# Transposing q and k by halves of the tokens, and reading a recurrent state with 64-row matmuls

## The chip, the cores and the metric

The kernel runs on one core of a Trainium2 chip. The metric is the time of one execution on the device, in microseconds (us); the median of five executions is given. A separate profiled execution of the same program gives the profile and the trace, on which all readings rest.

The core's engines work side by side: TensorE (PE; its weight loads are shown apart as PEld), VectorE (DVE), ScalarE (ACT), GpSimd (POOL) and SyncE (SP), which here only starts DMA transfers. PSUM is the memory that matmuls write; its banks are named psX, psZ, psWH and psO below.

## What is computed

A gated linear recurrence over 768 tokens for 4 batches of 8 heads with 48 dimensions, and behind it a two-layer network with a squared ReLU:

```python
for t in range(S):
    state = alpha[:, :, t, :, None] * state + np.einsum('bhd,bhe->bhde', k[:, :, t], v[:, :, t])
    y[:, :, t] = np.einsum('bhd,bhde->bhe', q[:, :, t], state)
x = y.transpose(0, 2, 1, 3).reshape(B * S, H * D)      # 3072 x 384
out = np.maximum(x @ w_in, 0.0) ** 2 @ w_out           # 384 -> 2048 -> 384
```

## The kernel before

The work is cut into 12 units of 256 tokens of one batch (line 354: the first 256 tokens of the four batches are units 0 to 3, the next are 4 to 7, and so on). The recurrence inside a unit is computed by chunks. Tokens lie in pairs: partition p holds tokens 2p and 2p+1 (index j), and the unit has two chunks c, the partitions 0 to 63 and 64 to 127, each with 128 tokens. A unit goes through these steps:

- `load` (493): alpha, k, q and v go from DRAM into RAW, 384 KB each. Most loads start on SyncE's queue. From unit 5 on each load waits for a step of the unit before (`BEHIND`, line 491): alpha for `ln`, k for the landing of the first transpose `tr0_`, q and v for that of the second, `tr1_`. From unit 4 on it also waits for the landing of the previous unit's q (line 988).
- `front` (673): logarithms of alpha, summed along the tokens by a matmul (`m1`), become the factors EK and EQ; k and q times these go into QKS (line 694, bfloat16, each head padded from 48 to 64, so that two heads fill 128 columns). QKS is then transposed into KQT, so that dimensions lie on partitions. Units 0 to 2 do it with TensorE and a copy out of PSUM; from unit 3 on two DMA transposes on SyncE's queue do it (line 721), one for k (a=0) and one for q (a=1), each of a 128 x 1024 source.
- `scores` (810): 32 matmuls of 64 x 64 tiles give k times q for each chunk, head and token pair (line 827), into psX and psZ. VectorE multiplies them with the causal mask into PM (line 840).
- `output` (846) with `output_mm` (751): psX collects the result. First, q times the state: chunk 0 reads the old state SBD, chunk 1 the middle state SMD. These are 16 matmuls of 128 rows and 64 columns of the array (line 764), a pair of heads at a time, 96 columns each; since two heads share the rows, the blocks of the state that mix them must be zero. For units 0 to 3 there is no old state, and 8 matmuls remain. Then 32 matmuls of 64 rows (line 771) add PM times v, chunk c from the row tile c, into chunk c's bank. In the same piece of TensorE's program stand the next unit's state products (`state_mm`, line 744).
- `state` (782): VectorE adds the state products of the first chunk to SBD (into TMP[0], line 797), and POOL or VectorE masks out the mixed blocks (by OWN, lines 799 and 801) into SMD. Then the second chunk is added (TMP[1], line 804) and scaled by the decay, with mixed blocks set to zero (806 and 808), into SBD. For units 0 to 3 the masking is done in one step (794).
- ScalarE copies psX into XBF (858). Units 4 to 10 transpose XBF by a DMA (879), the others by TensorE (873).
- `moe` (911): the first layer takes 48 matmuls of 256 columns (930), ReLU and squares run on ACT and DVE (938 to 952), and the second layer takes 32 matmuls of 384 columns (966); copies and stores follow (973 to 976).

No loop runs on the chip: a planner (`Program.schedule`, 101) orders every engine's instructions when the program is built. Each operation has an engine or a choice of engines, an assumed cost, a due time, and the buffers that it reads and writes; the planner plays these through and takes at each point the ready operation that is due first. Due times are a multiple of 13 us per unit, but for the first units they come from the tables FRONT, ATTN and DENSE (357 to 359). An operation waits at run time, on its engine's queue, for the operations it depends on, and all that is planned behind it on that engine waits with it. Where TensorE has nothing to do before the first second-layer matmul, matmuls with zeros fill in (1010).

Of the kernel before, what the change touches and what calls it, by code (L numbers as in the profile page):

```python
# [6 lines left out]
ALU = mybir.AluOpType  # L7
# [326 lines left out]
def bass_gla_recurrent__then__act_relu_squared_kernel(  # L334
# [22 lines left out]
    FRONT = {0: 0, 1: 15124, 2: 28243, 3: 27962, 4: 36918, 5: 52460}  # L357
    ATTN = {1: 12619, 2: 26150, 3: 37152, 4: 50460}
    DENSE = {0: 20223, 1: 32105, 2: 46275, 3: 57124, 11: 158500}
# [4 lines left out]
    TR_RING = "sp"  # L364
    LATE_STATE = (1, 2)
    BY_HEADS = (0,)
# [124 lines left out]
    BEHIND = {"a": "ln", "k": "tr0_", "q": "tr1_", "v": "tr1_"}  # L491
# [181 lines left out]
    def front(g):  # L673
# [19 lines left out]
        for a, E, key in ((0, EK, "ek"), (1, EQ, "eq")):  # L693
# [5 lines left out]

        for a in range(2):  # L700
            src = QKS[qs][:, a].rearrange("p j h d -> p (j h d)")
            if g < PE_TRANSPOSED:
                bank = psZ[:, a, :].bitcast(BF16)
                psk = [("ps", "Z", a)]

                def tr(pe, src=src, bank=bank):
                    for o in range(2 * NPR):
                        ins = pe.matmul(bank[:, o * 128:(o + 1) * 128], src[:, o * 128:(o + 1) * 128], IDENT[:],
                                        is_transpose=True)
                    return ins  # L710

                add("pe", tr, pe_ns(8, 128), p0 + 2500 + a, reads=[("qks", qs, a), ("ident",)], writes=psk,
                    name=f"tr{a}_{g}")
                dst = KQT[kt][:, a].rearrange("p j n s -> p (j n s)")
                add("dve", lambda e, dst=dst, bank=bank: e.tensor_copy(dst, bank[:, 0:1024]), dve_ns(1024, 2),  # L715
                    p0 + 3000 + a, reads=psk, writes=[("kqt", kt, a)], name=f"et{a}_{g}",
                    alts={"act": (lambda e, dst=dst, bank=bank: e.activation(dst, bank[:, 0:1024], AF.Copy),
                                  act_ns(1024))})
            else:
                dst = KQT[kt][:, a].rearrange("p j n s -> p (j n) s")  # L720
                add(TR_RING, lambda e, dst=dst, src=src: e.dma_start_transpose(dst, src), 1300, p0 + 2500 + a,
                    reads=[("qks", qs, a)], writes=[("kqt", kt, a)], name=f"tr{a}_{g}", dma=f"t{a}_{kt}", lag=1700)
# [319 lines left out]
```

## Time and profile before

| what | value |
|---|---|
| median of 5 executions | 180.24 us (179.4 to 180.63) |
| profiled execution | 180.24 us, of which 178.4 in the span from first to last instruction |
| first layer on TensorE (L930) | 576 matmuls of 256 columns, busy 74.5 us |
| second layer on TensorE (L966) | 368 matmuls of 384 columns, busy 69.0 us |
| state read (L764) | 160 matmuls, 128 x 64 of the array |
| PM times v (L771) | 384 matmuls, 64 x 128 of the array |
| DMA transposes of QKS (L721) | 18, landing 4.4 us after issue (median; 3.2 to 6.0) |
| loads of RAW | 2.7 to 6.8 us to landing, median 4.8 |

The profile's busy times add the full lengths of single matmuls, which overlap in TensorE's pipeline; what a group of matmuls takes of TensorE is read from the starts of the groups. The profile gives the DMA engines' load as a mean over all 16.

### The profile page before, as it was taken

The numbers are of one execution on the slowest core, as the hardware profiler recorded it, in microseconds if no ns is written. First come the engines' busy times: TensorE is split into PE (matmuls) and PEld (weight loads), VectorE is DVE, ScalarE is ACT, GpSimd is POOL, SyncE is SP. The second block draws the span as 40 slices with busy tenths as digits, with TensorE's granted clock in tenths as the row PEclk, the third lists the DMA queues.
The fourth block names the chain that finished last, engine by engine and source line by source line (L and its number), as shares of the span: only waits on it lengthen the run. The fifth ranks groups of instructions, "written<-read, shape, count | busy, mean of one in ns | idle before, by whom it ended". The sixth has DMA issues, their size and how long they took to land.

```text
span 178.4 us, 5228 instructions
## 1 busy us (share of the span) xinstructions
PE 171.8 (96%) x2287; PEld 136.6 (77%) x2287; DVE 121.4 (68%) x197; ACT 120.1 (67%) x211; POOL 25.8 (14%) x35
## 2 busy tenths in 40 slices
PE   7699899999999999999999999999999999999994
PEld 5577698866778689678878877878788697798773
DVE  6379589789968987869959937848858646342130
ACT  5566289686699786658779757858787664475541
POOL 3060654320002204001102110100100100000000
PEclk9999999999999999999999999999999999999999
DMA  4999999998999898879999997698979930110112
GB/s 123 251 324 185 209 331 208 218 253 242 225 272 215 231 175 208 240 163 212 224 256 201 194 288 183 142 287 121 237 193 241 216 94 5 44 48 0 44 48 88
DMA packets 74615, 33.18 MB, mean 186 GB/s; under 512 B 69888, under 2 KB 73088, under 8 KB 74592
## 3 DMA queue, kind: packets, MB, share of 16 engines
q1 hardware_dynamic: 72944, 27.73, 68.5%
q0 software_dynamic: 1648, 5.11, 12.8%
q8 instruction: 18, 0.29, 0.7%
q14 instruction: 5, 0.04, 0.1%
HBM read 25.17 MB, written 4.72 MB: 168 GB/s over the span
## 4 chain that ended last, share of the span: by engine, by line
PE 81%; DMA 11%; SPq 3%; ACT 2%; issue 1%; POOL 1%
PE psO L966 34%; PE psWH L930 33%; DMA raw<-in_alpha_dram 6%; DMA win<-in_moe_w_in_dram 5%; PE psX L771 3%; PE psX L764 2%; SPq L514 2%; PE psX L827 2%; PE psZ L744 2%; PE psX L900 1%; PE psZ L827 1%; PE psWH L632 1%; ACT gt L952 1%; POOL prd L625 1%; PE psX L873 1%
## 5 line engine op out<-in xcount | busy, mean ns | idle before, releaser
L930 PE MATMUL psWH<-xt,win 128*128 128x256 bf16 x576 | 74.5, 275 | 0.8 <-DMA win<-in_moe_w_in_dram 0.8
L930 PEld LDWEIGHTS psWH<-xt,win 128*128 128x128 bf16 x576 | 64.9, 145 | 6.0 <-DVE kqt L715 1.0
L966 PE MATMUL psO<-wout,gt 128*128 128x384 bf16 x368 | 69.0, 326 | 0.1
L938 ACT ACTIVATE rr<-psWH 128x512 bf16<-128x512 f32 x85 | 50.4, 595 | 25.6 <-PE psWH L930 24.4
L966 PEld LDWEIGHTS psO<-wout,gt 128*128 128x128 bf16 x368 | 35.3, 98 | 17.8 <-ACT osb L973 0.3
L948 DVE TENSOR_TENSOR gt<-rr 128x1024 bf16<-128x1024 bf16 (+1 forms) x43 | 24.2, 572 | 20.2 <-ACT rr L938 20.0
L973 ACT ACTIVATE osb<-psO 128x384 f32<-128x384 f32 x20 | 9.8, 490 | 11.0 <-PE psO L966 10.4
L952 ACT ACTIVATE gt<-rr 128x1024 bf16<-128x1024 bf16 (+1 forms) x17 | 15.8, 931 | 0.6 <-DVE rr L940 0.2
L840 DVE TENSOR_TENSOR pm<-psZ,caus 128x1024 bf16<-128x1024 f32 x12 | 14.6, 1216 | 2.1 <-PE psZ L827 2.1
L840 DVE TENSOR_TENSOR pm<-psX,caus 128x1024 bf16<-128x1024 f32 x12 | 14.6, 1218 | 1.5 <-PE psZ L827 1.5
L858 ACT ACTIVATE xbf<-psX 128x768 bf16<-128x768 f32 x11 | 8.9, 811 | 5.9 <-PE psZ L744 4.5
L1010 PE MATMUL psO<-zero 128*128 128x256 bf16 x72 | 11.1, 303 | 1.2 <-DVE zero L426 1.2
L690 POOL CAST vbf<-raw 128x768 bf16<-128x768 f32 x6 | 5.1, 847 | 43.6 <-DMA raw<-in_v_dram 43.6
L797 DVE TENSOR_TENSOR tmp<-psZ,sbd 128x384 f32<-128x384 f32 x8 | 4.5, 558 | 10.2 <-PE psZ L744 10.1
L694 DVE TENSOR_TENSOR qks<-raw,eq 128x768 bf16<-128x768 f32 x11 | 10.5, 953 | 1.2 <-DMA raw<-in_q_dram 0.6
L694 DVE TENSOR_TENSOR qks<-raw,ek 128x768 bf16<-128x768 f32 x11 | 10.5, 951 | 0.6 <-DMA raw<-in_k_dram 0.6
L1010 PEld LDWEIGHTS psO<-zero 128*128 128x128 bf16 x72 | 7.4, 108 | 2.7 <-DVE zero L426 1.2
L940 DVE TENSOR_SCALAR rr<-psWH 128x512 bf16<-128x512 f32 x11 | 7.5, 686 | 1.7 <-PE psWH L930 1.6
L771 PE MATMUL psX<-vbf,pm 64*128 64x48 bf16 x384 | 6.9, 180 | 0.0
L806 POOL TENSOR_TENSOR sbd<-tmp,acm 128x384 bf16<-128x384 f32 x4 | 4.2, 1048 | 18.3 <-DVE tmp L804 18.1
L653 DVE TENSOR_TENSOR ek<-ek,raw 128x384 f32<-128x384 f32 x9 | 6.0, 668 | 0.9 <-ACT ek L644 0.7
L644 ACT ACTIVATE ek<-psWH 128x384 f32<-128x384 f32 x10 | 4.9, 490 | 2.0 <-PE psWH L636 2.0
(120 smaller groups left out, 164.8 us busy)
## 6 DMA issues: line engine op xcount, KB each, us to landing
out_dram<-osb SPq DMA_DIRECT2D x23, 192.0 KB, 2.9
raw<-in_k_dram SPq DMA_DIRECT2D x11, 384.0 KB, 4.3
raw<-in_q_dram SPq DMA_DIRECT2D x11, 384.0 KB, 4.8
raw<-in_v_dram SPq DMA_DIRECT2D x10, 384.0 KB, 5.7
raw<-in_alpha_dram SPq DMA_DIRECT2D x10, 384.0 KB, 4.4
win<-in_moe_w_in_dram POOLq DMA_DIRECT2D x2, 768.0 KB, 9.7
wout<-in_moe_w_out_dram POOLq DMA_DIRECT2D x2, 768.0 KB, 9.3
raw<-in_v_dram POOLq DMA_DIRECT2D x2, 384.0 KB, 6.3
```

Source lines behind the costliest of these rows:

```text
L694: add("dve", lambda e, a=a, E=E: e.tensor_tensor(QKS[qs][:, a, :, :, 0:D], RAW[r][:, 1 + a].rearrange("p h j d -> p j h d"), E[la][:].rear ...
L771: ins = pe.matmul(psX[:, c, h * D:(h + 1) * D], PM[pm][64 * c:64 * c + 64, n // 2, rr_, n % 2, jk, :], VBF[vb][64 * c:64 * c + 64, h, jk, ...
L840: add("dve", lambda e, hf=hf, psT=psT: e.tensor_tensor(PM[pm][:, hf].rearrange("p r n j t -> p (r n) (j t)"), psT[:, :, :].rearrange("p r ...
L858: add("act", lambda e: e.activation(XBF[x2][:], psX[:, :, 0:HD], AF.Copy), act_ns(2 * HD), p0 + 6100, reads=[("ps", "X", 0), ("ps", "X", 1 ...
L930: ins = pe.matmul(psH[hb][:, i * T:(i + 1) * T], WIN[:, kk, hidden(fj)], mov, start=(kk == 0), stop=(kk == KT - 1))
L938: add("act", lambda e, hb=hb, rr=rr: e.activation(rr, psH[hb], AF.Relu), act_ns(512), pu + 600, reads=[("ps", "H", hb)], writes=[("rr", rb ...
L940: alts={"dve": (lambda e, hb=hb, rr=rr: e.tensor_scalar(rr, psH[hb], 0.0, None, ALU.max), dve_ns(512))})
L948: add("dve", lambda e, dst=dst, sq=sq: e.tensor_tensor(dst, sq, sq, ALU.mult), 148 + k * 267, pu + 1200, reads=[("rr", rb, h) for h in ran ...
L952: "act": (lambda e, dst=dst, sq=sq: e.activation(dst, sq, AF.Square), act_ns(k * 512))})
L966: ins = pe.matmul(psS, GT[gt][:, fj, j, :], WOUT[:, fj, :], start=(fj == 0), stop=(fj == FT - 1))
L973: add("act", lambda e, ob=ob, psS=psS: e.activation(OSB[ob][:], psS, AF.Copy), act_ns(DM), ps_ + 700, reads=[keyS], writes=[("osb", ob)], ...
L1010: pr.fill(lambda pe: pe.matmul(psO[:, 0:256], ZERO[:, 0:128], ZERO[:, 0:256], skip_group_check=True), 109, min(o.start for o in pr.order[" ...
```

## The change

From unit 3 on (`ROW_TILED`):

- The two DMA transposes of a unit each take 64 partitions (one chunk, c) of both k and q: a source of 64 x 2048 in place of 128 x 1024. So both wait for the products of k and of q.
- q is multiplied by its factor in two instructions, one for each j, and laid out so that the transposed q of one chunk and head pair are 128 neighbouring columns.
- The scores read from the new places. Shapes and count stay.
- q times the state becomes 64-row matmuls, a head at a time, 48 columns each, that fill all 128 columns of the array. Row tile x holds the heads 2p+x. [...]the step is cut in two: head parity x writes chunk c = x first; then come the 32 products with v and the next unit's state products; then TensorE waits on a semaphore of its own for the last product with v, and parity x writes chunk c = 1 - x.
- The mixed blocks of SMD are no longer read, so the masking of SMD goes, and the sum is written to SMD directly (for unit 3 a copy). TMP is chosen by the parity of the unit.
- Loads of k wait for the previous unit's product of k (`ekm`), those of q and v for the first of its transposes.
- The due times of units 0 to 5 in FRONT, ATTN and DENSE are changed.

```diff
-    FRONT = {0: 0, 1: 15124, 2: 28243, 3: 27962, 4: 36918, 5: 52460}
-    ATTN = {1: 12619, 2: 26150, 3: 37152, 4: 50460}
-    DENSE = {0: 20223, 1: 32105, 2: 46275, 3: 57124, 11: 158500}
+    FRONT = {0: 0, 1: 13357, 2: 25644, 3: 26390, 4: 37530, 5: 53567}
+    ATTN = {1: 14618, 2: 26767, 3: 37301, 4: 52103}
+    DENSE = {0: 19639, 1: 32250, 2: 48764, 3: 61983, 11: 158500}
...
-    BEHIND = {"a": "ln", "k": "tr0_", "q": "tr1_", "v": "tr1_"}
+    BEHIND = {"a": "ln", "k": "ekm", "q": "tr0_", "v": "tr0_"}
...
+        for j in range(2) if g in ROW_TILED else ():
+            dst = QKS[qs][:, 1].rearrange("p j h d -> p (j h d)").rearrange("p (n j x d) -> p j n x d", n=NPR, j=2, x=2)[:, j, :, :, 0:D]
+            add("dve", lambda e, j=j, dst=dst: e.tensor_tensor(
+                dst, RAW[r][:, 2, :, j, :].rearrange("p (n x) d -> p n x d", x=2),
+                EQ[la][:, j].rearrange("p (n x d) -> p n x d", n=NPR, x=2), ALU.mult),
+                dve_ns(HD), p0 + 1600 + j, reads=[("raw", r, 2), ("eq", la, j)], writes=[("qks", qs, 1, j)], name=f"eqm{j}_{g}")
...
+        if g in ROW_TILED:
+            for c in range(2):
+                src = QKS[qs][64 * c:64 * c + 64].rearrange("p a j h d -> p (a j h d)")
+                dst = transposed(kt, c).rearrange("p (b s) -> p b s", s=64)
+                add("sp", lambda e, dst=dst, src=src: e.dma_start_transpose(dst, src), 1300, p0 + 2500 + c,
+                    reads=[("qks", qs, 0), ("qks", qs, 1)], writes=[("kqt", kt, 0, c), ("kqt", kt, 1, c)], name=f"tr{c}_{g}",
+                    dma=f"t{c}_{kt}", lag=1700)
+            return
...
-                dst = KQT[kt][:, a].rearrange("p j n s -> p (j n) s")
-                add(TR_RING, lambda e, dst=dst, src=src: e.dma_start_transpose(dst, src), 1300, p0 + 2500 + a,
-                    reads=[("qks", qs, a)], writes=[("kqt", kt, a)], name=f"tr{a}_{g}", dma=f"t{a}_{kt}", lag=1700)
...
+    def transposed(kt, c):
+        return KQT[kt][:].rearrange("p a j n s -> p (a j n s)")[:, c * 1024:c * 1024 + 1024]
+
+    def queries(kt, c, n):
+        return transposed(kt, c)[:, 512 + n * 128:512 + n * 128 + 128]
...
+    def output_row_tiled(g, between, between_ns):
...
+        def states(pe, tiles):
+            for p in range(NPR):
+                for x, c in tiles:
+                    h = 2 * p + x
+                    ins = pe.matmul(psX[:, c, h * D:h * D + D], queries(kt, c, p)[64 * x:64 * x + 64],
+                                    (SMD[x2] if c else SBD[sr])[64 * x:64 * x + 64, h * D:h * D + D],
+                                    start=(p == 0 and x == c), stop=False, skip_group_check=True)
+            return ins
+
+        def run(pe):
+            states(pe, ((1, 1),) if first else ((0, 0), (1, 1)))
+            for h in range(H):
...
+            ins.then_inc(swap, 1)
+            swaps[0] += 1
+            if between:
+                between(pe)
+            pe.wait_ge(swap, swaps[0])
+            return states(pe, ((0, 1),) if first else ((0, 1), (1, 0)))
...
+        if g in ROW_TILED and first:
+            add("dve", lambda e: e.tensor_copy(SMD[x2][:], ps0), dve_ns(HD), p0 + 2900,
+                reads=[key0], writes=[("smd", x2)], name=f"sa{g}",
+                alts={"act": (lambda e: e.activation(SMD[x2][:], ps0, AF.Copy), act_ns(HD))})
+        elif g in ROW_TILED:
+            add("dve", lambda e: e.tensor_tensor(SMD[x2][:], ps0, SBD[sr][:], ALU.add), dve_ns(HD),
+                p0 + 2900, reads=[key0, ("sbd", sr)], writes=[("smd", x2)], name=f"sa{g}")
...
-            add("dve", lambda e: e.tensor_tensor(TMP[0][:], ps0, SBD[sr][:], ALU.add), dve_ns(HD),
-                p0 + 2900, reads=[key0, ("sbd", sr)], writes=[("tmp", 0)], name=f"sa{g}")
-            add("pool", lambda e: e.tensor_tensor(sm3, hd(TMP[0][:]), own, ALU.mult), pool_ns(HD), p0 + 3200,
-                reads=[("tmp", 0), ("own",)], writes=[("smd", x2)], name=f"sb{g}",
-                alts={"dve": (lambda e: e.tensor_tensor(sm3, hd(TMP[0][:]), own, ALU.mult), dve_ns(HD))})
...
-            add("dve", lambda e: e.tensor_tensor(TMP[1][:], ps1, SMD[x2][:], ALU.add), dve_ns(HD),
-                p0 + 3600, reads=[key1, ("smd", x2)], writes=[("tmp", 1)], name=f"sc{g}")
+            add("dve", lambda e: e.tensor_tensor(TMP[g % 2][:], ps1, SMD[x2][:], ALU.add), dve_ns(HD),
+                p0 + 3600, reads=[key1, ("smd", x2)], writes=[("tmp", g % 2)], name=f"sc{g}")
```

## The prediction

> **What bounds the kernel now.** I read, in this order, busy time and slices, the chain that ended last, TensorE's instructions in order of time, then SyncE's queue and the DMA engines.
>
> ```profile
> span 178.4 us, 5228 instructions
> PE 171.8 (96%) x2287; PEld 136.6 (77%) x2287; DVE 121.4 (68%) x197; ACT 120.1 (67%) x211; POOL 25.8 (14%) x35
> ...
> PE   7699899999999999999999999999999999999994
> ...
> DMA  4999999998999898879999997698979930110112
> ...
> PE 81%; DMA 11%; SPq 3%; ACT 2%; issue 1%; POOL 1%
> ```
>
> TensorE has no free slice after the first few, and it holds 81% of the chain that ended last. The DMA engines are nearly as full until slice 31 (about 138 us). So a change counts at full size where it shortens TensorE's own stream, and a change that lengthens a transfer can turn the bound around. One steady period on TensorE, in order of time (start us, length us, line, output from inputs, count):
>
> ```profile
> 101.73 2.76 PE L966 MATMUL psO<-wout,gt 128*128 128x384 bf16 x16
> 104.42 0.36 PE L764 MATMUL psX<-sbd,kqt 128*64 128x96 bf16 x8
> 104.62 0.34 PE L764 MATMUL psX<-smd,kqt 128*64 128x96 bf16 x8
> 104.89 0.58 PE L771 MATMUL psX<-vbf,pm 64*128 64x48 bf16 x32
> 105.30 0.50 PE L744 MATMUL psZ<-vbf,qks 64*128 64x96 bf16 x8
> 105.73 0.44 PE L930 MATMUL psWH<-xt,win 128*128 128x256 bf16 x2
> ```
>
> Lengths overlap, so prices are taken from starts. The previous output step began at 91.68, so a period is 104.42 - 91.68 = 12.74 us. In the chain of waits 12 of L930 take 1.31 us (0.109 each) and 16 of L966 take 2.60 (0.1625 each), so the dense layers need 48 x 0.109 + 32 x 0.1625 = 10.4 us of it; the attention gets 2.3. The output step is the larger part. L966 is through at 101.73 + 2.60 = 104.33. Then: 0.09 to change the array's form, 0.20 for eight products with the old state, 0.27 for eight with the middle state and a second change of form (104.62 to 104.89), 0.41 for 32 products with v (12.8 ns each), 0.43 for 16 state products and the change back. That is 1.40 us.
>
> Before 66.5 us TensorE also waits. I add the dense work between 19.39 us (first L930) and 66.50 as 168 x 0.109 + 96 x 0.1625 = 33.9, and the attention's in the same way, about 10; of the 47.1 us some 3.2 are waits and fill. Before 19.39 it waits for the first weights (DMA win, 11.06 to 19.25 in the chain), which the change doesn't touch.
>
> **What the Trainium skill says.** "TensorEngine Tiling (Array Packing)", Key Properties: changing the tiling mode drains the engine. The trace agrees: 0.07 to 0.09 us where the form changes. Its Gotcha 1 says that different row tiles cannot use one PSUM bank at the same time; that explains the new wait between the two halves of the state products, and nothing in this trace shows it (in L771 each row tile has its own bank). "TensorE: Matmul & The Clock Gate", Architectural detail, gives a queue of 64 instructions that pulls weight loads ahead: the 16 state products (32 instructions) fit there while the sequencer stands at the wait. "DMA: Bandwidth & Descriptors", Rules for kernel authors: transfers of two partition halves use the same 16 engines, so the split gains no bandwidth; its section on silent corruption speaks of 256-byte source rows. The packets agree: 72944 of q1 less 42 x 1024 + 2 x 512 (loads) and 25 x 128 (stores) leave 25712 for 25 transposes, 1.08 for each such row.
>
> **The change, part by part.**
>
> State products (units 3 to 11). Removed for a unit with an old state: 16 matmuls of 128 x 64 and one change of form, 0.20 + 0.27 = 0.47. Added: 16 matmuls of 64 rows x 128 x 48 columns on alternating row tiles. That is L771's shape, so 16 x 12.8 ns = 0.205. Saved 0.265 us. Unit 3 has no old state: 8 products and a change, 56.03 to 56.32 (0.29), become 8 x 12.8 = 0.10; saved 0.19.
>
> The swap wait. It stands after the v products and the next unit's state products, and asks for the last v product. A L771 lasts 179 ns, and a release reaches PE in 0.05 us (ACT acm ends at 29.88, the weight load that waits for it starts at 29.93), so it opens 0.23 us after that product starts. The state products between keep the array busy 0.34. I take 0, and between 0 and 0.2 for the range (below nothing is excluded: a wait gives no time). Behind it stand the second half of the state products and all later matmuls; XBF and the state sums wait for these, and end earlier as long as the bubble is below 0.265. Unit 11 has nothing between: its bubble is 0.23 to 0.25 against 0.265 saved, so zero.
>
> Sum on TensorE: units 4 to 10 give 7 x 0.265 = 1.86, unit 3 0.19, unit 11 0.02: **2.07 us**; with a bubble of 0.1 in eight units 1.25.
>
> Scores: the same 32 matmuls, now from contiguous columns. L708 streams 128 contiguous columns in 219 ns, L827 its strided 128 in 216; taken as 0, with 3 ns x 32 = 0.1 us a unit as the bound to either side.
>
> VectorE, from these rows:
>
> ```profile
> L694 DVE TENSOR_TENSOR qks<-raw,eq 128x768 bf16<-128x768 f32 x11 | 10.5, 953 | 1.2 <-DMA raw<-in_q_dram 0.6 <-POOL eq L660 0.3 <-ACT eq L670 0.2
> L801 DVE TENSOR_TENSOR smd<-tmp,own 128x384 bf16<-128x384 f32 x6 | 3.3, 557 | 0.2
> L799 POOL TENSOR_TENSOR smd<-tmp,own 128x384 bf16<-128x384 f32 x2 | 1.7, 828 | 12.2 <-DVE tmp L797 12.2
> ```
>
> The mask of the middle state goes (8 times: 6 x 557 ns on DVE, 2 x 828 on POOL). The product of q becomes two of 384 elements, 2 x 557 for 953: +160 ns in 9 units. Net about -1.9 us of VectorE over the run. It is worth nothing on the path: VectorE is busy 9.1 us of a steady 12.77 and no steady matmul waits for it.
>
> SyncE and DMA. Steady order now (start, issue time):
>
> ```profile
> 98.85 1.23 SPq L721 DMA_TRANSPOSE kqt<-qks  x1
> 100.13 1.06 SPq L514 DMA_DIRECT2D raw<-in_alpha_dram  x1
> 101.23 0.58 SPq L976 DMA_DIRECT2D out_dram<-osb  x1
> 101.85 1.39 SPq L721 DMA_TRANSPOSE kqt<-qks  x1
> 103.28 0.65 SPq L514 DMA_DIRECT2D raw<-in_k_dram  x1
> 105.05 0.36 SPq L976 DMA_DIRECT2D out_dram<-osb  x1
> 106.67 1.21 SPq L879 DMA_TRANSPOSE xt<-xbf  x1
> 107.93 0.58 SPq L514 DMA_DIRECT2D raw<-in_q_dram  x1
> ```
>
> The first transpose started after the product of k; now both need k and q, so it moves from 98.85 to about 101. The load of k now follows that product, not a landing, and moves ahead of both transposes. Loads of q and v follow the first landing instead of the second. With a median landing of 4.4 us, the pair lands at about 107, as now; with a k load ahead of it (a load lands in 4.8) perhaps 109. The scores that read it stand at 98 + 12.7 = 110.6. This move is worth 0 while those 2 to 4 us of cover last. A transpose's price: q1 is busy 68.5% x 178.4 = 122.2 us on 72944 packets, 26.8 ns each on 16 engines, so 1024 of them cost an estimated 1.7 us of all engines, 3.4 per unit. A 64 x 2048 source has the same 1024 rows of 256 bytes, so I take the same price; half the partitions on the reading side could make it twice that at worst, and no reason is seen for a gain above 10%.
>
> Start-up. The due times of units 1 to 5 change, so the planner's order between 15 and 66 us does. It can win at most the 3.2 us of waits and could lose as much; taken as 0, with 1 each way for the ordinary case.
>
> Forecast: the profiled execution took 180.24 us, 1.84 outside its span, and is also the median. 180.24 - 2.07 = **178.2 us**, own range 177.0 to 179.3.
>
> **Rivals.**
>
> Exposed swap. The array runs dry at each swap because weight loads behind the wait start only when it opens. For: PE shows "issue" idle at 9 starts of L764, where a wait and a change of form meet. Against: 0.34 us of cover for 0.23 of latency. With 0.2 in eight units, 2.07 - 1.6 = 0.47 remain: 179.8.
>
> Slower transposes, the case on the other side. Place: each unit's pair on the DMA engines, from unit 4 on.
>
> ```profile
> 91.68:104.42 12.74, 12.74 (x178) 10.16 (x177) 9.32 (x13) 9.32 (x16) 2.03 (x2) 1.00 0.98 222
> 104.42:117.20 12.78, 12.78 (x170) 10.13 (x169) 8.62 (x12) 9.63 (x17) 1.69 (x2) 1.00 0.86 198
> 117.20:130.00 12.80, 12.80 (x171) 10.13 (x170) 9.45 (x15) 9.19 (x17) 0.83 (x1) 1.00 1.00 205
> ```
>
> The DMA share (second last column) of three steady periods is 0.98, 0.86 and 1.00, about 12.1 us in 12.77. At 1.5 times, a pair adds 1.7: 13.8 against a new period of 12.5, 1.3 in each of eight units; 4.4 us of cover go first, so 178.2 + 10.4 - 4.4 = 184.2. It decides from a price of about 1.3 times, and at twice it would give 198. Against it: the equal count of rows, and that this share counts queued packets, so the engines are less full than it says.
>
> Worse start. Unit 3's scores (52.69) follow its second transpose (issued 47.38) closely; if the later pair and the new order leave TensorE 2 us more idle there, 180.2, with 3 us 181.2.
>
> Better start: half of the 3.2 us of waits go, 176.6.
>
> **How the numbers follow.** Forecast 0.62, exposed swap 0.12, slower transposes 0.10, worse start 0.11 (0.06 within half a percent, 0.05 slower), better start 0.05. Half a percent (0.9 us) is what a measurement of this kernel can tell, so the lines are 179.3 and 181.1. Faster: 0.62 + 0.05 + a few of the swap case at a smaller bubble (0.03) = 0.70. Slower: 0.15. Within: 0.15. The range 176.6 to 180.7 leaves out the transposes, the slower starts and little else.
>
> **What would show it.** Right: an output step of about 1.13 us with its changes of form, a period near 12.5, no idle before the second half of the state products, landings of 4 to 6 us. Wrong: PE idle at the swap, DMA releasers ahead of L827, a period at or above 12.74, or a first L764-like step of unit 4 later than 66.5.

## The result, and the profile after

The changed kernel takes 179.86 us (median of 27 runs, 177.49 to 183.09), the kernel before 179.79 beside it (48 runs, 178.75 to 182.07). The ratio is **0.9971, with a 95% interval of 0.9949 to 0.9992**: some 0.5 us faster by this ratio, a quarter of the 1.1% forecast. The prediction's 178.2 us, against its 180.24, is a ratio of 0.9887, which lies outside the interval. Ratios leave out executions more than 1.5% above the fastest of their kernel, for the changed kernel nine of 28 (180.70 us and more, at full clock), while medians take all in, and by these the two kernels take the same time.

The profiled execution of the changed kernel took 180.06 us, close to its median. The page:

```profile
span 178.3 us, 5220 instructions
PE 169.4 (95%) x2287; PEld 135.2 (76%) x2287; DVE 121.3 (68%) x205; ACT 120.7 (68%) x214; POOL 16.0 (9%) x25
...
DMA  4999999999999797899897898699998592110112
...
PE 58%; DMA 19%; DVE 8%; issue 6%; ACT 4%; SPq 3%; POOL 1%; POOLq 0%; DVEq 0%
```

TensorE is busy 2.4 us less than before, yet the span is shorter by only 0.1. In the chain that ended last, TensorE has fallen from 81% to 58%, DMA has grown from 11% to 19%, and VectorE, absent before, has 8%. So the work left TensorE, and waits took its place.

First, that the saving is there. TensorE's instructions around the output step of unit 6, in order of time (start us, length us, line, output from inputs, count):

```profile
91.98 0.19 PE L781 MATMUL psX<-sbd,kqt 64*128 64x48 bf16 x1
...
92.09 0.56 PE L792 MATMUL psX<-vbf,pm 64*128 64x48 bf16 x32
92.50 0.50 PE L760 MATMUL psZ<-vbf,qks 64*128 64x96 bf16 x16
92.83 0.18 PE L781 MATMUL psX<-smd,kqt 64*128 64x48 bf16 x1
...
93.03 0.44 PE L992 MATMUL psWH<-xt,win 128*128 128x256 bf16 x2
```

From the first state read to the first layer's next matmul: 93.03 - 91.98 = 1.05 us. Before it was 105.73 - 104.42 = 1.31. The second half of the state reads (92.83) starts where the state products end, with no idle time in front. Four periods from one output step to the next (length; then each engine's busy time; PE clock, DMA share, GB/s last):

```profile
91.98:104.46 12.48, 12.48 (x179) 10.01 (x179) 10.73 (x18) 9.45 (x17) 0.00 (x0) 1.00 1.00 217
104.46:116.94 12.48, 12.48 (x172) 10.01 (x171) 8.95 (x14) 9.39 (x16) 0.00 (x0) 1.00 0.84 195
116.94:130.02 13.08, 12.70 (x171) 9.93 (x171) 10.33 (x18) 9.15 (x17) 0.00 (x0) 1.00 1.03 226
130.02:143.01 12.99, 12.54 (x170) 10.00 (x171) 9.01 (x14) 8.92 (x16) 0.00 (x0) 1.00 0.86 173
```

Two periods are 12.48 us, 0.26 to 0.32 below the 12.74 to 12.80 of before. The next two are 13.08 and 12.99: 0.6 and 0.5 us are gone again. What TensorE waited for (total us, times, longest), four of the five lines that the kernel before doesn't have (the fifth, 0.3 us at 12.24, lies in the start-up):

```profile
PE psX L821 <- DVE qks L700: 0.7, 1, 0.7
PE psX L781 <- ACT vbf L691: 0.4, 1, 0.4
PE psWH L992 <- DMA xt<-xbf: 0.4, 1, 0.4
PE psX L781 <- POOL vbf L690: 0.3, 1, 0.3
```

1.8 us in all. L821 is the output step of unit 2, at 43.46: VectorE made the first half of unit 3's product of q (L695) ahead of its product of k, which the state products in the same piece of TensorE's program need. The two vbf lines are copies of v that ended late because v was loaded late, and L992 waits for the transpose of x. SyncE's queue through one period of the changed kernel (start, issue time):

```profile
115.35 4.29 SPq L711 DMA_TRANSPOSE kqt<-qks  x2
119.68 1.53 SPq L1038 DMA_DIRECT2D out_dram<-osb  x2
121.27 1.24 SPq L941 DMA_TRANSPOSE xt<-xbf  x1
122.56 0.72 SPq L514 DMA_DIRECT2D raw<-in_q_dram  x1
123.33 0.58 SPq L514 DMA_DIRECT2D raw<-in_v_dram  x1
126.33 0.37 SPq L514 DMA_DIRECT2D raw<-in_alpha_dram  x1
126.75 0.58 SPq L514 DMA_DIRECT2D raw<-in_k_dram  x1
127.77 5.27 SPq L711 DMA_TRANSPOSE kqt<-qks  x2
```

Read it as a loop. Each step starts 0.04 to 0.06 us after the one before, but for 2.4 us ahead of alpha (which waits for q's landing) and 0.4 ahead of the transposes. So the loop is made of issue times and of one landing. From pair to pair it takes 127.77 - 115.35 = 12.42 us, and the next q follows at 135.50, 12.94 after the last one. TensorE needs 12.48. The 18 transposes of q and k hold this queue 38.5 us in all, 30.3 before.

### The profile page after: what moved, and what is told of

It reads as the page before. It is cut to its first block, busy times and chain, and to the rows that moved or that the text cites. A ratio compares the mean times of both kernels' runs of the same rounds, so it can differ in the third digit from the quotient of the medians.

```text
span 178.3 us, 5220 instructions
## 1 busy us (share of the span) xinstructions
PE 169.4 (95%) x2287; PEld 135.2 (76%) x2287; DVE 121.3 (68%) x205; ACT 120.7 (68%) x214; POOL 16.0 (9%) x25
## 3 DMA queue, kind: packets, MB, share of 16 engines
q1 hardware_dynamic: 72944, 27.73, 68.3%
## 4 chain that ended last, share of the span: by engine, by line
PE 58%; DMA 19%; DVE 8%; issue 6%; ACT 4%; SPq 3%; POOL 1%; POOLq 0%; DVEq 0%
PE psWH L992 25%; PE psO L1028 22%; DMA raw<-in_alpha_dram 6%; DMA win<-in_moe_w_in_dram 4%; DMA raw<-in_v_dram 3%; DMA raw<-in_q_dram 3%; SPq L514 3%; DVE pm L900 2%; DMA xt<-xbf 2%; PE psX L792 2%; ACT rr L1000 2%; PE psZ L760 2%; PE psX L781 1%; PE psX L962 1%; PE psX L889 1%
## 5 line engine op out<-in xcount | busy, mean ns | idle before, releaser
L992 PE MATMUL psWH<-xt,win 128*128 128x256 bf16 x576 | 73.6, 274 | 1.3 <-DMA win<-in_moe_w_in_dram 0.8
L992 PEld LDWEIGHTS psWH<-xt,win 128*128 128x128 bf16 x576 | 65.2, 145 | 6.1 <-DVE kqt L730 0.8
L1000 ACT ACTIVATE rr<-psWH 128x512 bf16<-128x512 f32 x82 | 47.9, 593 | 21.6 <-PE psWH L992 20.5
L1010 DVE TENSOR_TENSOR gt<-rr 128x1024 bf16<-128x1024 bf16 (+1 forms) x39 | 22.8, 587 | 21.0 <-ACT rr L1000 20.9
L1014 ACT ACTIVATE gt<-rr 128x1024 bf16<-128x1024 bf16 (+1 forms) x21 | 18.3, 873 | 0.6
L695 DVE TENSOR_TENSOR qks<-raw,eq 128x384 bf16<-128x384 f32 x18 | 9.3, 554 | 7.5 <-DMA raw<-in_q_dram 7.5
L691 ACT ACTIVATE vbf<-raw 128x768 bf16<-128x768 f32 x8 | 6.7, 842 | 7.3 <-DMA raw<-in_v_dram 7.1
L1002 DVE TENSOR_SCALAR rr<-psWH 128x512 bf16<-128x512 f32 x14 | 9.6, 686 | 0.9 <-PE psWH L992 0.6
L666 ACT ACTIVATE la<-raw 128x384 f32<-128x384 f32 x8 | 4.2, 522 | 4.9 <-DMA raw<-in_alpha_dram 4.9
L623 DVE TENSOR_TENSOR prd<-raw 128x384 f32<-128x384 f32 x8 | 4.4, 556 | 3.0 <-DMA raw<-in_alpha_dram 2.9
L760 PE MATMUL psZ<-vbf,qks 64*128 64x96 bf16 x144 | 5.6, 202 | 0.0
```

The costliest lines, as they stand in the source:

```text
L695: add("dve", lambda e, j=j, dst=dst: e.tensor_tensor(dst, RAW[r][:, 2, :, j, :].rearrange("p (n x) d -> p n x d", x=2), EQ[la][:, j].rearr ...
L760: ins = pe.matmul(banks[c][:, p * 96:p * 96 + 96], QKS[qs][h0:h0 + 64, 0, j, 2 * p:2 * p + 2, :].rearrange("p h d -> p (h d)"), VBF[vb][h0 ...
L992: ins = pe.matmul(psH[hb][:, i * T:(i + 1) * T], WIN[:, kk, hidden(fj)], mov, start=(kk == 0), stop=(kk == KT - 1))
L1000: add("act", lambda e, hb=hb, rr=rr: e.activation(rr, psH[hb], AF.Relu), act_ns(512), pu + 600, reads=[("ps", "H", hb)], writes=[("rr", rb ...
L1002: alts={"dve": (lambda e, hb=hb, rr=rr: e.tensor_scalar(rr, psH[hb], 0.0, None, ALU.max), dve_ns(512))})
L1010: add("dve", lambda e, dst=dst, sq=sq: e.tensor_tensor(dst, sq, sq, ALU.mult), 148 + k * 267, pu + 1200, reads=[("rr", rb, h) for h in ran ...
```

## The experiments

Ratios are to the kernel before, run beside each, with the 95% interval. Changing an operation lets the planner order all engines anew, so a small difference between two versions may be the order alone (neighbours in the table further below differ by 0.1 to 0.3%). The letters that name theories are those of each text.

**The two parts apart.** The changed transposes, loads and due times, with the state reads of before (128 x 64) and their masks:

```diff
...
-        if g in ROW_TILED:
-            run, cost, reads, writes = output_row_tiled(g, run2, cost2)
...
+                                  queries(kt, c, p)[:, 64 * j:64 * j + 64] if g in ROW_TILED else
...
```

> The changed kernel with the 128 x 64 state products and the masks of before, reading the new layout. Theory A (the new transposes and load order cost about 1.5 us by late loads, the matmuls save 2): with TensorE's slower period of 12.75 most late loads are covered again, so 0 to 0.8 us slower than before, and PE waits for v or xt under 1 us. Theory B (the matmuls save nothing in the run): the same time as the changed kernel, 0.5 us faster than before. Theory C (the new order of the first 66 us costs the 1.5 us): 1.0 to 1.5 us slower than before, with the first output step of an old state later than 66.5.

Measured: 1.0116 (1.0089 to 1.0142). This part alone costs about 2.1 us, more than any of the theories gave. In its trace TensorE is idle for 1.5 us between 66.25 and 92.59, of which 1.32 are one wait for x's transpose, at 75.61; from 92.59 to 144.25 it has no gap. With the longer step of before, the steady periods have room for the halves.

The row-tiled reads alone, with everything else as before; they read columns of neighbouring tokens, so the state products are of other tokens at the same size:

```diff
...
-        return transposed(kt, c)[:, 512 + n * 128:512 + n * 128 + 128]
+        return KQT[kt][:, 1, c, n, :]
...
```

> Before's transposes, products of q, loads and due times; only the output step is row-tiled and the masks are gone. The stationary columns are 128 neighbouring ones of KQT that belong to other tokens, so the state products are of the wrong tokens; counts and shapes are those of the change. Theory A: 1.5 to 2.1 us faster than before, the full saving less what the old loads already lack. Theory B: 0 to 0.6 us faster. Theory D (the loads were at their pace before the change already, so any faster TensorE runs into them): 0.3 to 1.0 us faster, with waits for v or xt in the trace.

Measured: 0.9927 (0.9902 to 0.9951), about 1.3 us faster: less than theory A gave, and not the forecast's 0.9887. So the matmuls bring time and the transposes with their loads take it. The two don't add up to the 0.9971 of both (the changes of 1.0116 and 0.9927 would sum to 1.0043); why not stays open.

**The swap.** The state products moved behind the second half of the state reads, so that nothing covers the wait:

```diff
-            if between:
-                between(pe)
             pe.wait_ge(swap, swaps[0])
-            return states(pe, ((0, 1),) if first else ((0, 1), (1, 0)))
+            ins = states(pe, ((0, 1),) if first else ((0, 1), (1, 0)))
+            if between:
+                ins = between(pe)
+            return ins
```

> The changed kernel with the next unit's state products behind the second half of the state read, so that nothing covers the swap wait. By the prediction's latency the wait opens 0.23 us after the last product with v starts, so a bubble of 0.2 to 0.25 in each of units 3 to 10: 1.6 to 2.0 us slower than the changed kernel if TensorE sets the time everywhere, 0.5 to 1.2 if late loads take the place of part of it. If the change's wait is exposed already (theory B), no slower than the changed kernel.

Measured: 1.0097 (1.0071 to 1.0124). Weight loads of this version, from the list of costliest groups:

```profile
L781 PEld LDWEIGHTS psX<-smd,kqt 64*128 64x128 bf16 x72 | 2.9, 93 | 1.7 <-PE psX L792 1.5 <-issue 0.2
```

1.5 us of idle time behind L792, the last product with v, in nine units: 0.17 each. The step itself, from the first state read (104.97) to the first layer (106.25), takes 1.28 us in place of 1.05, which is 0.23 a unit, and three of its four steady periods are 12.72. In the changed kernel the same row has 0.2 of idle time in all, so the cover holds there. The swap is not where the time went.

**Due times, loads, and the order in unit 3.** The tables of before in the changed kernel; then the loads' places of before; then two places further ahead; last, unit 3's product of q behind that of k.

```diff
-    FRONT = {0: 0, 1: 13357, 2: 25644, 3: 26390, 4: 37530, 5: 53567}
+    FRONT = {0: 0, 1: 15124, 2: 28243, 3: 27962, 4: 36918, 5: 52460}
...
```

> The changed kernel with before's FRONT, ATTN and DENSE. Theory C (the new due times of the first 66 us lose): 0.5 to 1.5 us faster than the changed kernel. If they gain, as much slower. Theory A says nothing of them: within 0.5, and still waits of TensorE for v or xt after 75 us.

```diff
-    BEHIND = {"a": "ln", "k": "ekm", "q": "tr0_", "v": "tr0_"}
+    BEHIND = {"a": "ln", "k": "tr0_", "q": "tr1_", "v": "tr1_"}
```

> The changed kernel with before's rule for the loads: k behind the landing of the first transpose, q and v behind the second. Theory A1 (the load of k ahead of the transposes on SyncE's queue is what delays xt, q and v): 0.3 to 1.0 us faster than the changed kernel, transposes in pairs under 3.6 us on SyncE. Theory A2 (the transposes are late because both wait for both products): q and v start later still, 0.5 to 2 us slower than the changed kernel.

```diff
+    BEHIND = {"a": "ln", "k": "ekm", "q": "ekm", "v": "ekm"}
```

> The changed kernel with loads of q and v behind the previous unit's product of k, not behind the landing of its first transpose. Theory A: the waits for v and xt go, 0.8 to 1.5 us faster than the changed kernel (1.3 to 2.0 faster than before), as long as the transposes behind two more loads still land before the scores. Theory B: no change against the changed kernel, within 0.3. Theory E (the DMA engines are full, so an order only moves the wait): waits move to the scores or xt, within 0.5 of the changed kernel.

```diff
+    BEHIND = {"a": "ln", "k": "ekm", "q": "tr0_", "v": "ekm"}
```

> The changed kernel with the load of v behind the product of k, ahead of the transposes, and q as in the change. In the changed kernel TensorE waits 0.30 us (78.3) and 0.45 us (142.6) for the copy of v. Theory A: these waits go and the transposes and xt have cover for it, 0.5 to 1.0 us faster than the changed kernel. Theory E (the queue is full, a transfer moved ahead delays the next by as much): the waits move to xt or to the scores, 0 to 3 us slower.

```diff
...
-                dve_ns(HD), p0 + 1600 + j, reads=[("raw", r, 2), ("eq", la, j)], writes=[("qks", qs, 1, j)], name=f"eqm{j}_{g}")
+                dve_ns(HD), p0 + 1600 + j, reads=[("raw", r, 2), ("eq", la, j)] + ([("qks", qs, 0)] if g == 3 else []), writes=[("qks", qs, 1, j)], name=f"eqm{j}_{g}")
```

> The changed kernel, but in unit 3 the product of q waits for that of k. In the changed kernel's trace VectorE does one half of q's product (0.55 us) before k's in unit 3, and TensorE's output step of unit 2, which holds unit 3's state products, waits 0.70 us for k's product at 43.46. If this wait is on the path, 0.4 to 0.6 us faster than the changed kernel (0.7 to 0.9 faster than before), with that idle at 0.3 or less. If later waits for loads (v, xt) set the time in any case, within 0.2 of the changed kernel.

Measured: old due times 0.9991 (0.9969 to 1.0013), old places of the loads 0.9993 (0.9972 to 1.0013), the order in unit 3 0.9951 (0.9921 to 0.9981). All three overlap with the changed kernel, so none of them is shown to be the cause. Loads further ahead are clearly worse, where theory A had them faster: q and v behind `ekm` 1.0258 (1.0218 to 1.0298), v alone 1.0273 (1.0227 to 1.0318). In the latter TensorE waits 3.6 us for KQT: the load that goes ahead of the transposes delays them by more than the scores have room for. That points to SyncE's queue, or to the DMA engines behind it.

**Is it the queue?** The changed kernel with its stores of units 3 to 10 issued from GpSimd's queue, some 1.5 us per unit off SyncE's; and, as a control, the kernel before with the same edit.

```diff
-            add("sp", lambda e, ob=ob, rows=rows: e.dma_start(out[rows, :], OSB[ob][:]), 600, ps_ + 1300,
+            ring, cost = ("pool", 930) if 3 <= g <= 10 else ("sp", 600)
+            add(ring, lambda e, ob=ob, rows=rows: e.dma_start(out[rows, :], OSB[ob][:]), cost, ps_ + 1300,
...
```

> The changed kernel with the two stores of each of units 3 to 10 issued by GpSimd's queue instead of SyncE's; 16 instructions of about 0.75 us leave SyncE's queue, so its loop of transposes, stores, loads and x's transpose gets some 1.5 us shorter per unit. Theory A (SyncE's queue, a loop of 12.5 to 13.2 us per unit, is what gives the saved matmul time back): v, x's transpose and k's product come earlier, TensorE's waits for v (0.30 and 0.45 us) and for x's transpose (0.38) shrink, and the time falls 0.5 to 1.2 us below the changed kernel, ratio to the kernel before 0.990 to 0.995. Rival E (the 16 DMA engines themselves are short, wherever their work is issued): within 0.3 us of the changed kernel, 0.9955 to 0.9985.

> The kernel before with the same stores on GpSimd's queue, a control. Theory A: TensorE's period of 12.8 us leaves its SyncE queue slack, so nothing changes: ratio 0.998 to 1.002. Rival (the queue already set the pace of the kernel before): 0.990 to 0.996.

Measured: 0.9914 (0.9877 to 0.9950) for the changed kernel, within what theory A gave. The control came out at 1.0086 (1.0058 to 1.0114), which neither side expected: in the kernel before, the move costs 1.5 us, by a way that was not followed up. It does show that moving stores is no gain in itself. The changed kernel's own gain by it is 0.6%, with intervals that just overlap (0.9950 and 0.9949). Periods of the changed kernel with its stores on GpSimd, in its profile of 178.15 us, its median:

```profile
91.19:103.71 12.52, 12.52 (x178) 9.97 (x178) 9.60 (x15) 9.97 (x18) 1.08 (x2) 1.00 1.01 222
103.71:116.19 12.48, 12.48 (x170) 9.99 (x171) 9.35 (x15) 10.10 (x18) 1.08 (x2) 1.00 0.99 209
116.19:128.67 12.48, 12.48 (x170) 10.00 (x171) 9.10 (x14) 9.53 (x17) 1.08 (x2) 1.00 1.00 216
128.67:141.15 12.48, 12.48 (x170) 10.01 (x170) 9.24 (x14) 9.14 (x17) 1.08 (x2) 1.00 1.03 176
```

All four are TensorE's own period, at a DMA share (second last column) of 0.99 to 1.03. A full DMA share is therefore no bound by itself. The opposite test lengthens the queue at equal bytes: each store as two of 64 rows, both on SyncE.

```diff
+            for hh in range(2) if 3 <= g <= 10 else (None,):
+                src = OSB[ob][:] if hh is None else OSB[ob][64 * hh:64 * hh + 64]
+                dst = out[rows, :] if hh is None else out[rows, :][64 * hh:64 * hh + 64]
...
```

> The changed kernel with each store of units 3 to 10 issued as two of 64 rows on SyncE: the same bytes, packets and work of the 16 DMA engines, but some 1.2 us more of SyncE's queue in every unit. Theory A (the queue's loop sets the pace): 1 to 6 us slower than the changed kernel, ratio to the kernel before 1.003 to 1.03. Rival E (the DMA engines, not the queue): within 0.4 us of the changed kernel, 0.995 to 0.9995.

Measured: 1.0190 (1.0112 to 1.0268), some 4 us slower than the changed kernel, though the size is rough, from six executions. Its fastest run is the one profiled:

```profile
90.59:103.64 13.05, 12.06 (x173) 9.23 (x173) 9.20 (x15) 9.52 (x18) 0.00 (x0) 1.00 0.93 187
103.64:116.58 12.94, 12.54 (x169) 9.93 (x170) 8.42 (x13) 9.45 (x17) 0.83 (x1) 1.00 0.89 196
116.58:129.53 12.95, 12.55 (x170) 9.93 (x170) 8.44 (x13) 9.62 (x17) 0.83 (x1) 1.00 0.98 209
129.53:143.28 13.75, 12.62 (x170) 9.93 (x171) 8.52 (x13) 10.11 (x18) 0.83 (x1) 1.00 0.90 186
```

No period is below 12.94, while the DMA share is lower than in the version above. So a longer queue at equal bytes lengthens the periods, which the DMA engines' share doesn't explain. The queue's loop holds a landing as well, however, so these two versions don't tell its issue times from the landings that it waits for.

**What fills the queue: halves, split product or joint wait?** Four versions with the row-tiled matmuls, the new due times and loads. Where a version's transposes or product differ from the changed kernel's, scores or state products read columns of other tokens or heads, at the same size. Whole transposes with one product of q each wait for their own product (e15), or for both (e14), or for both with the product split (e17); e16 has halves and one product.

```diff
...
-            for c in range(2):
-                src = QKS[qs][64 * c:64 * c + 64].rearrange("p a j h d -> p (a j h d)")
+            for a in range(2):
+                src = QKS[qs][:, a].rearrange("p j h d -> p (j h d)")
...
```

> The changed kernel's matmuls, masks, due times and load placements, but q's product in one instruction and the transposes of the kernel before, 128 rows by 1024, the one of k waiting only for k's product and the one of q only for q's. The output step reads columns of neighbouring tokens, so its state products are of the wrong tokens at the same size. Theory A: k's transpose starts about 0.6 us before q's product is done and the pair takes about 3.4 us of the queue instead of 4.3, so the loop is shorter: 0.6 to 1.3 us faster than the changed kernel, ratio 0.989 to 0.994. Rival (the loads' new places or the new due times give the saved time back, not the transposes): as the changed kernel, 0.995 to 0.999.

> As e15, but both transposes wait for both products, as the halves must (the row-tiled step again reads neighbouring tokens' columns). If the joint wait is the cost: as the changed kernel, 0.995 to 0.999, and 0.6 us or more slower than e15. If the shape of the transposes or the split product is the cost: as e15 within 0.3 us.

> The changed kernel, transposes by halves, with q's product in one instruction; q's columns stand in the order of the kernel before, so scores and state products read columns of other heads and tokens, at the same size. If the split product (two instructions of VectorE in place of one, per unit) is the cost: 0.986 to 0.990, as the version with whole transposes and a joint wait. If the halves themselves are: 0.995 to 0.999, as the changed kernel.

> The version with whole transposes that both wait for both products, now with q's product in two instructions as in the changed kernel; columns of other heads and tokens are read, at the same size. If the split product is the cost: 0.995 to 0.999. If the halves are: 0.986 to 0.990.

Measured, with both transposes waiting for both products unless stated:

| transposes | q's product split | q's product in one |
|---|---|---|
| halves, 64 x 2048 | 0.9971 (0.9949 to 0.9992), the changed kernel | 1.0003 (0.9973 to 1.0032) |
| whole, 128 x 1024 | 0.9906 (0.9880 to 0.9932) | 0.9874 (0.9835 to 0.9913) |
| whole, each waiting for its own | | 0.9887 (0.9843 to 0.9931) |

The rows differ, the columns don't. The halves cost (0.9971 + 1.0003)/2 - (0.9906 + 0.9874)/2 = 0.97%, or 1.7 us; the split product and the joint wait cost nothing that these runs can tell. The expectation that the joint wait was the price fell. The version with whole transposes and a split product (e17) differs from the changed kernel in the shape of the transposes alone, apart from which columns are read; three of its steady periods:

```profile
103.44:115.92 12.48, 12.48 (x172) 10.01 (x171) 9.74 (x15) 9.37 (x16) 0.00 (x0) 1.00 0.84 203
115.92:128.40 12.48, 12.48 (x171) 10.00 (x171) 9.74 (x15) 9.49 (x16) 0.00 (x0) 1.00 1.04 229
128.40:140.88 12.48, 12.48 (x172) 10.01 (x171) 9.27 (x14) 8.32 (x14) 0.00 (x0) 1.00 0.87 177
```

Its span is 2.1 us shorter than that of the changed kernel's trace: 0.5 are won ahead of unit 4's output step (65.00 against 65.55), 0.5 in the next two periods, and 1.1 in the four from unit 6 to unit 10 (49.92 against 51.03). Its SyncE queue:

```profile
112.39 4.09 SPq L711 DMA_TRANSPOSE kqt<-qks  x2
116.52 1.06 SPq L1037 DMA_DIRECT2D out_dram<-osb  x2
117.91 1.45 SPq L940 DMA_TRANSPOSE xt<-xbf  x1
119.41 0.57 SPq L514 DMA_DIRECT2D raw<-in_q_dram  x1
```

Between the stores' end (117.58) and x's transpose the queue stands idle for 0.33 us, and one unit earlier for 0.95: it waits for ScalarE's copy of psX (ends at 105.40 and 117.88, 0.03 ahead of the transposes), which follows TensorE. So the queue has slack here. The same gap can be read in the other traces, for the six transposes of x between 64 and 140 us. With halves it never exceeds 0.06 us in the changed kernel, in e16, with old due times, with the old places of the loads, with k first, or with halved stores. In each of the three versions with whole transposes it is 0.24 to 1.33 us in at least four of the six, and in the version with the stores on GpSimd, which has halves, 0.66 to 0.98 in three. How long the transposes hold the queue tells the shapes apart less well (ns, min/median/max; the changed kernel, e17, e15):

```profile
L711 SPq DMA_TRANSPOSE kqt<-qks x18: 1241/2034/3254, 45.2 to 142.1; - x18
L711 SPq DMA_TRANSPOSE kqt<-qks x18: 1237/1394/3211, 44.9 to 138.5; - x18
L711 SPq DMA_TRANSPOSE kqt<-qks x18: 1239/2160/3092, 43.2 to 136.5; - x18
```

In all they hold it 38.5, 31.1 and 37.7 us, and the last belongs to whole transposes in a version as fast as e17. One profile doesn't decide alone either: that of e16 has 178.43 us where its 22 runs have a median of 180.16, and it shows periods of 12.48 although its queue has no slack. That the halves bring the queue to its edge, so that some executions lose by it and some don't, is a reading that no run shows.

**The price of a half by itself.** Nothing but transposes on an idle core, each pair waiting for the landing of the one before, in one execution without a planner: first 12 pairs, whole and halves in turn, then 12 pairs behind a load of k. The recurrence and the layers are left out.

```diff
+            f = halves if i % 2 else whole
+            for x in range(2):
+                f(e, i, x).then_inc(sems[i], 16)
+            e.wait_ge(sems[i], 32)
```

> Nothing but transposes: 12 pairs on an otherwise idle core, whole and halves in turn, then 12 pairs each behind a load of k (384 KB) on the same queue; the output is written for 128 rows alone and the rest of the computation is left out. If the halves themselves are dearer: from the first issue to the second landing a pair of halves takes 0.3 to 0.8 us longer than a pair of whole ones, alone and behind a load. If they cost the same and only their place among the other transfers differs: equal within 0.1 us in both stretches.

SyncE's queue (start, issue time; L365 whole, L370 halves):

```profile
3.42 2.71 SPq L365 DMA_TRANSPOSE kqt<-qks  x2
7.95 3.14 SPq L370 DMA_TRANSPOSE kqt<-qks  x2
13.41 2.61 SPq L365 DMA_TRANSPOSE kqt<-qks  x2
17.85 3.14 SPq L370 DMA_TRANSPOSE kqt<-qks  x2
23.54 2.61 SPq L365 DMA_TRANSPOSE kqt<-qks  x2
```

Two of these stretches as windows (length; clock, DMA share and GB/s last):

```profile
13.41:17.85 4.44, 0.00 (x0) 0.00 (x0) 1.00 0.61 118
17.85:23.54 5.69, 0.00 (x0) 0.00 (x0) 1.00 0.58 92
```

And each line's instructions in the first 75 us, of which one pair of each kind stands behind a load (duration in ns, and time from issue to landing; min/median/max):

```profile
L365 SPq DMA_TRANSPOSE kqt<-qks x14: 1232/1324/1839, 3.4 to 65.7; - x14
...
DMA to landing us min/median/max: 3.1/3.2/4.2
...
L370 SPq DMA_TRANSPOSE kqt<-qks x14: 1241/1580/2047, 7.9 to 71.4; - x14
...
DMA to landing us min/median/max: 3.7/4.0/4.4
```

From start to start a pair of whole transposes takes 4.4 to 4.5 us, a pair of halves 5.5 to 5.7: 1.24 times. They hold the queue 2.61 and 3.14 us (1.20 times). The DMA engines are busy 0.61 x 4.44 = 2.7 us for the one, 0.58 x 5.69 = 3.3 for the other, at the same bytes. Behind a load the stretches, with the load's issue, are 5.4 to 5.6 and 6.1 to 6.5 long, while the pairs hold the queue 3.1 to 3.3 and 3.2 to 3.7. So the halves are dearer in themselves, alone by more than the 0.3 to 0.8 us expected, and behind a load the difference lies in the landing more than in the issue.

**Combinations of edits shown above.** Stores on GpSimd with unit 3's product of k first; and stores on GpSimd with the old due times.

> The changed kernel with unit 3's product of q after that of k and the stores of units 3 to 10 on GpSimd's queue. Theory A (SyncE's queue was full, and the order of VectorE in unit 3 cost up to 0.7 us once): 0 to 0.6 us below the kernel with the stores moved alone, ratio to the kernel before 0.988 to 0.9915. Rival (the order in unit 3 doesn't reach the end): 0.991 to 0.993.

> The changed kernel with the stores of units 3 to 10 on GpSimd's queue and the due times of the kernel before. If the new due times are worth something of their own once the queue has slack: slower than with the stores moved alone, ratio to the kernel before 0.992 to 0.997. If they are worth nothing either way: 0.989 to 0.9925.

Measured: 0.9924 (0.9894 to 0.9954) and 0.9970 (0.9944 to 0.9997). The order in unit 3 adds nothing to 0.9914. The due times seem to: with slack in the queue, the old ones lose some 1.0 us, the whole of what the moved stores had gained, though the intervals overlap a little (0.9950 and 0.9944). With the old due times, moving the stores brings nothing that can be told (0.9991 to 0.9970). The best version that computes the output in full is the changed kernel with its stores on GpSimd: 178.15 us, 0.9914 of the kernel before. Against the changed kernel that is 0.9914/0.9971, or 0.6% less.

## Why the prediction was wrong, point by point

- *State products, "Saved 0.265 us".* Right: 1.31 to 1.05 us in the step, 12.74 to 12.48 in an unhindered period.
- *"The swap wait ... I take 0."* Right. No idle in front of the second half; uncovered, the step is 0.23 us longer, as the prediction's latency gave it. The version without cover lost 1.26% against the changed kernel, 2.3 us, and nine times 0.23 are 2.1.
- *Scores, taken as 0.* Nothing against it: with 12.48 the saved 0.26 us is the whole difference.
- *VectorE, "Net about -1.9 us ... worth nothing on the path".* The busy time stayed at 121 us, for the planner moved other work there while GpSimd's fell from 25.8 to 16.0. It is off the path in the steady units, but not in unit 3, where q's first half went ahead of k's product and TensorE waited 0.70 us at 43.46. That wait was not foreseen; putting k first did not bring a time that can be told from the changed kernel's.
- *SyncE and DMA, "A 64 x 2048 source has the same 1024 rows of 256 bytes, so I take the same price".* **This is the step that failed.** Rows and bytes are the same, the price is not: alone, a pair of halves takes 1.24 times as long to land and 1.20 times as long on the queue, and in the kernel the halves cost 0.97%, 1.7 us, where the prediction put nothing. The page of the changed kernel hid it: 72944 packets as before, q1 at 68.3% of the span against 68.5%, a median landing of 4.6 us against 4.4. Only the shortest landings, 3.7 against 3.2 us, showed a step.
- *"This move is worth 0 while those 2 to 4 us of cover last."* The cover was counted at one place, the scores. But the pair stands in a queue with stores, the transpose of x and the loads of the next unit behind it. These have readers of their own (v's copy, the first layer). In the kernel before, the copy of unit 11's v ended at 142.07, for unit 10's output step, which holds unit 11's state products, at 142.81:

```profile
141.24 0.83 POOL L690 CAST vbf<-raw 128x768 bf16<-128x768 f32 x1 [13.14 <-DMA raw<-in_v_dram]
142.81 0.36 PE L764 MATMUL psX<-sbd,kqt 128*64 128x96 bf16 x8
```

That is 0.74 us of room, the least of the steady units (1.8 to 2.3 in the three before it), and not 2 to 4. A queue that is passed through once a unit has as cover the period less its own length with its waits, and the change took from both: the period fell by 0.26 us, and the queue's slack ahead of x's transpose, up to 1.26 us in the kernel before, went to 0.06 and less.
- *Rival "slower transposes", "It decides from a price of about 1.3 times".* The mechanism is the right one, but it decided at 1.2, not 1.3: the 4.4 us of cover that the prediction set against the loss were not there. It did not reach the 184.2 that it gave for 1.5 times.
- *Start-up, "taken as 0, with 1 each way".* Within its bounds: the new due times are worth 0.2% where the queue is full and 0.6% where it isn't (the intervals overlap in both cases).

With whole transposes the forecast comes out: its ratio of 0.9887 lies in all three intervals of the versions with them. What was missing from the sum was a cost of about 1.7 us for the halves. That the total then agrees with 0.9887 is in part luck: the row-tiled matmuls alone, with all else as before, reached only 0.9927, with an interval that leaves 0.9887 out, and those three versions have the new due times too, which were taken as 0. The sum for TensorE is shown for the single step and the unhindered period, not for the whole run. That the halves' cost goes by way of SyncE's queue is supported by the gaps ahead of x's transpose and by the two versions with moved and halved stores; how much of it is issue time and how much later landings is not separated. The Trainium skill has the sign to look for: "Perfetto Trace Analysis", What "DMA-bound" means, names the issuing engine's sequencer as a bound of its own, one whose track is solid DMA slices; and DMA Optimizations there says that balancing over the engines that can issue may help. The trace agrees in part: from 114.22 to 136.69 SyncE's track has no gap longer than 0.06 us but those ahead of alpha (2.4 us, a wait for q's landing) and of the transposes, so it binds without being solid, and the move of the stores brought 0.6%.

What stays open: why halves are dearer at equal rows and bytes of the source (they differ from whole transposes in the partitions read, 64 against 128, and also in the blocks written, 64 columns wide against 128, which no run tells apart); why the stores' move costs the kernel before 0.9%; and why the two parts alone don't add up.

## What to carry to other kernels

Before TensorE's period is shortened, lay out the queue that issues the transfers as a loop, with every issue time and every wait on a landing, and compare its length with the new period; cover is to be read at each reader of each transfer that stands behind the changed one. Equal bytes, rows and packets don't make two shapes of a DMA transpose equal: price the new shape by a small run of its own.

## What the runs showed of the hardware

- Two DMA transposes of 64 x 2048 (bfloat16) against two of 128 x 1024: 5.5 to 5.7 against 4.4 to 4.5 us to the landing of the pair, 3.14 against 2.61 us of the issuing queue, on an idle core; behind a 384 KB load 6.1 to 6.5 against 5.4 to 5.6 us from the load's issue on.
- A DMA share of 0.99 to 1.03 over four periods stood beside a TensorE without a gap (12.48 us each); shares of 0.89 to 0.98 stood beside periods of 12.94 to 13.75.
- A store of 64 rows held SyncE's queue as long as one of 128 (0.59 us at 109.02 in the version with halved stores, 0.58 at 83.57 in the changed kernel), and doubling the number of stores at equal bytes made the kernel about 4 us slower.
- A wait for the last product with v, with nothing to cover it, lengthened the output step by 0.23 us (1.28 against 1.05); with the 16 state products between, no idle time was left.
